# First Wk chunk loaded ahead of the third and fourth x tiles, with key matmuls of the first chunk between the transposes

## The chip, the cores and the metric

The kernel runs on one core of one Trainium2 chip. The metric is the device time of one execution in microseconds (us). The *span* in a profile is the time from the first to the last instruction of one execution; here it is about 2 us less than the device time of the same run.

## The reference, cut to what matters

```python
x = A_x                                          # 1 x 2048 x 512, bf16
g = sigmoid((x * gate_w).sum(-1))
a = linear_attention(x, wqkv, wo)                # 32 heads of 16; k = x @ Wk, pk = phi(k)
b = token_mlp(layernorm(x), w1, b1, w2, b2)      # mixes along the 2048 rows
out = g * a + (1 - g) * b
```

Only the start of the kernel matters here. It computes `k = x @ Wk` for the first row tiles of x. A tile is 128 rows, and there are 16. The contraction length of 512 is cut into four chunks of 128, so one tile needs four key matmuls, one per chunk of Wk, and all four need the tile transposed.

Of the kernel before, what the change touches and what calls it, by code (L numbers as in the profile page):

```python
# [15 lines left out]
def kernel(  # L16
# [13 lines left out]
    nc = tc.nc  # L30
# [10 lines left out]
    ND = D // P  # L41
# [25 lines left out]
    def bank(name, dtype=FP32):  # L67
        return ps.tile([P, SC], dtype, name=name, tag="bank")
# [39 lines left out]
    def mm(o, lhsT, rhs, start, stop, **kw):  # L108
        nc.tensor.matmul(o, lhsT=lhsT, rhs=rhs, start=start, stop=stop, **kw)  # L109
# [14 lines left out]
    def load_x(q, t0, n):  # L124
        q.dma_start(out=xs[:, t0 : t0 + n, :], in_=x_view[:, t0 : t0 + n, :])  # L125

    def load_wk(q, k):
        q.dma_start(out=wk_sb[:, k, :], in_=wqkv_view[:, k, D : 2 * D])
# [3 lines left out]
            out=xT[:, :, t0 * P : (t0 + n) * P], in_=X[t0 * P : (t0 + n) * P, :], transpose=True  # L132
        )

    for i in range(2):
        load_x(nc.sync, 2 * i, 1)
        load_x(nc.scalar, 2 * i + 1, 1)
    for i in range(2):
        load_wk(nc.sync, 2 * i)
        load_wk(nc.scalar, 2 * i + 1)  # L140
    NPE = 6
    load_x(nc.sync, 4, 2)
    for t0, n in ((NPE, 2), (8, 4), (12, 4)):
# [42 lines left out]
    def warm_up(n, cols=SC):  # L186
        for _ in range(n):
            mm(wps[:, :cols], warm[:, 0:P], warm[:, :cols], True, True)
# [5 lines left out]
    def transpose_tile(t, on_act):  # L194
        pt = bank("pt", BF16)
        for k in range(ND):
            nc.tensor.transpose(pt[:, k * P : (k + 1) * P], xs[:, t, k * P : (k + 1) * P], ident[:])  # L197
        dst = xT[:, :, t * P : (t + 1) * P]
        src = pt[:].rearrange("p (k s) -> p k s", k=ND)
        if on_act:  # L200
            nc.scalar.activation(out=dst, in_=src, func=ACT.Copy)
        else:
            nc.vector.tensor_copy(out=dst, in_=src)  # L203
# [13 lines left out]
    def k_part(t, ks):  # L217
        if t not in kaccs:
            kaccs[t] = bank("kacc")
        for k in ks:  # L220
            mm(
                kaccs[t][:], xT[:, k, t * P : (t + 1) * P], wk_sb[:, k, :],
                k == 0, k == ND - 1,
            )
# [4 lines left out]
    def ln_stats(t):  # L229
        stats = work.tile([P, nc.vector.BN_STATS_DIM], FP32, name="stats", tag="stats", bufs=2)  # L230
        nc.vector.bn_stats(out=stats[:], in_=xs[:, t, :])  # L231
        nc.vector.bn_aggr(out=mv[:, t, :], in_=stats[:])

    def ln_rstd(g):
        s = slice(g * TPC, (g + 1) * TPC)
        nc.vector.tensor_scalar_add(out=veps[:, s], in0=mv[:, s, 1], scalar1=EPS)
        nc.gpsimd.tensor_tensor(out=rstd[:, s], in0=veps[:, s], in1=mhalf[:], op=ALU.pow)
# [39 lines left out]
    def ln_step(u):  # L277
        ln_stats(u)
        if u % TPC == TPC - 1:
            ln_rstd(u // TPC)  # L280

    HEADS = 4
    transpose_tile(0, False)
    transpose_tile(1, True)
    warm_up(1, 256)
    transpose_tile(2, False)
    transpose_tile(3, True)
    ln_step(0)
    ln_step(1)
    for k in range(ND - 1):  # L290
        for t in range(HEADS):
            k_part(t, (k,))
    for t in range(HEADS):
        k_part(t, (ND - 1,))
        if t == 1:
# [210 lines left out]
```

## The kernel before: the parts that the change touches

```python
def load_x(q, t0, n): ...      # rows of x, 128 KB per tile
def load_wk(q, k): ...         # chunk k of Wk, 128 KB

for i in range(2):
    load_x(nc.sync, 2 * i, 1)          # SP queue:     x0, x2, wk0, wk2, then x4+x5, ...
    load_x(nc.scalar, 2 * i + 1, 1)    # scalar queue: x1, x3, wk1, wk3
for i in range(2):
    load_wk(nc.sync, 2 * i)
    load_wk(nc.scalar, 2 * i + 1)
load_x(nc.sync, 4, 2)
# ... all further loads on the SP queue

warm_up(6)                             # six 512-column matmuls on constants
HEADS = 4
transpose_tile(0, False)               # 4 transposes on PE, copy to xT by VectorE
transpose_tile(1, True)                # ... copy to xT by ScalarE
warm_up(1, 256)
transpose_tile(2, False)
transpose_tile(3, True)
ln_step(0); ln_step(1)                 # layernorm statistics, VectorE
for k in range(ND - 1):                # chunk-major: chunk 0 for tiles 0..3, chunk 1, chunk 2
    for t in range(HEADS):
        k_part(t, (k,))
for t in range(HEADS):                 # chunk 3
    k_part(t, (ND - 1,))
    if t == 1:
        transpose_tile(HEADS, False)
for t in range(HEADS):
    k_phi(t)                           # ScalarE exp, two VectorE operations -> pk
for t in range(HEADS, NT):
    k_part(t, range(ND))
    if t + 1 < NPE:                    # NPE = 6
        transpose_tile(t + 1, True)
    k_phi(t)
    g_tile(t - LAG)                    # 4 matmuls that use pk: "gacc" in the profile
    # ... layernorm pieces
```

I call the part up to the last of these first 16 key matmuls the *head*. The tile names in the profile are `wps` (warm-up), `pt` (transposes), `kacc` (key matmuls), `gacc` (the next matmuls, which use pk) and `zacc` (a short group of 16 matmuls after the last key tile). "Chunk 0" is `wk0` and "tile 3" is `x3`.

## Time and profile before

| | before |
|---|---|
| time, median of the first 3 runs | 168.21 us (167.87 to 168.40) |
| span of the profiled run | 166.4 us |
| PE busy | 97% of the span |
| wait of PE for the first Wk chunk | 0.41 us |
| first `gacc` matmul | 11.05 us |

The page of the kernel before gives the span, the busy time of each engine, and the chain of work that ended last by engine and by line:

```profile
span 166.4 us, 2105 instructions
...
PE 161.7 (97%) x806; PEld 74.9 (45%) x806; DVE 80.2 (48%) x190; ACT 59.0 (35%) x91; POOL 18.2 (11%) x37
...
PE 94%; DMA 3%; DVE 1%; SPq 0%; issue 0%
```

PE is the limit. The 3% DMA is at the very start. This is the timeline of PE alone; the columns are start, duration, engine, line, operation with tiles and shapes, count, and in brackets the idle time before the group and what ended it:

```profile
0.84 2.72 PE L109 MATMUL wps<-const-bfloat16-1.0 128*128 128x512 bf16 x6 [0.84 <-PEq L490]
3.62 1.03 PE L197 MATMUL pt<-ident,xs 128*128 128x128 bf16 x8
4.44 0.42 PE L109 MATMUL wps<-const-bfloat16-1.0 128*128 128x256 bf16 x1
4.66 0.96 PE L197 MATMUL pt<-ident,xs 128*128 128x128 bf16 x8
6.03 3.18 PE L109 MATMUL kacc<-wk_sb,xT 128*128 128x512 bf16 x14 [0.41 <-DMA wk_sb<-in_A_wqkv_dram]
...
11.05 1.23 PE L109 MATMUL gacc<-pk,xs 128*128 128x512 bf16 x4
```

All four tiles are transposed before the first key matmul. Then PE waits for chunk 0. From 6.03 the matmuls go out one every 0.216 us: the 14 of the group take 3.18 us, of which 0.38 is the last one's own duration, and (3.18 - 0.38) / 13 = 0.215. The chain of waits before says which load it was; the columns are start, duration and what:

```profile
1.72 4.26 DMA wk_sb<-in_A_wqkv_dram
5.99 0.04 issue
6.03 3.18 PE kacc L109 x14
```

Chunk 0 is third on the SP queue, is issued at 1.72 us and lands at 5.98 us.

### The profile page before, as it was taken

The numbers are of one execution on the slowest core, as the hardware profiler recorded it, in microseconds if no ns is written. First come the engines' busy times: TensorE is split into PE (matmuls) and PEld (weight loads), VectorE is DVE, ScalarE is ACT, GpSimd is POOL, SyncE is SP. The second block draws the span as 40 slices with busy tenths as digits, with TensorE's granted clock in tenths as the row PEclk, the third lists the DMA queues.
The fourth block names the chain that finished last, engine by engine and source line by source line (L and its number), as shares of the span: only waits on it lengthen the run. The fifth ranks groups of instructions, "written<-read, shape, count | busy, mean of one in ns | idle before, by whom it ended". The sixth has DMA issues, their size and how long they took to land.

```text
span 166.4 us, 2105 instructions
## 1 busy us (share of the span) xinstructions
PE 161.7 (97%) x806; PEld 74.9 (45%) x806; DVE 80.2 (48%) x190; ACT 59.0 (35%) x91; POOL 18.2 (11%) x37
## 2 busy tenths in 40 slices
PE   7999999999999999999999999999999999999992
PEld 3544444444544444444444444444444444444461
DVE  1569999986986769992301504051222121111121
ACT  3272474827658557222222111051111222111110
POOL 5000602100020000002712521000000000000000
PEclk9999999999999999999999999999999999999999
DMA  5999999999700001910597499931100000110001
GB/s 155 257 181 274 345 352 347 348 349 338 186 0 2 0 0 55 357 33 32 188 293 194 140 336 274 313 127 64 35 32 32 32 33 32 47 51 32 32 32 32
DMA packets 28953, 24.78 MB, mean 149 GB/s; under 512 B 6736, under 2 KB 28368, under 8 KB 28944
## 3 DMA queue, kind: packets, MB, share of 16 engines
q1 hardware_dynamic: 26928, 21.76, 45.0%
q0 software_dynamic: 1440, 2.38, 5.0%
q10 hardware_dynamic: 576, 0.52, 1.0%
q8 instruction: 6, 0.10, 0.3%
q14 instruction: 3, 0.02, 0.0%
HBM read 21.11 MB, written 2.23 MB: 140 GB/s over the span
## 4 chain that ended last, share of the span: by engine, by line
PE 94%; DMA 3%; DVE 1%; SPq 0%; issue 0%
PE uacc L109 29%; PE yps L109 29%; PE gacc L109 8%; PE qacc L109 8%; PE aps L109 8%; PE kacc L109 8%; DMA wk_sb<-in_A_wqkv_dram 3%; PE zacc L109 1%; PE denps L109 1%; PE kvps L109 1%; PE wps L109 1%; SPq L125 0%; DVE ot L471 0%; PE pt L197 0%; DVE xT L203 0%
## 5 line engine op out<-in xcount | busy, mean ns | idle before, releaser
L109 PE MATMUL uacc<-hs,w1c 128*128 128x512 bf16 x224 | 52.0, 379 | 0.0
L109 PE MATMUL yps<-uT,w2c 128*128 128x512 bf16 (+1 forms) x238 | 51.0, 367 | 0.0
L109 PEld LDWEIGHTS <-w2c 128*128 128x128 bf16 x238 | 23.3, 98 | 25.3
L109 PEld LDWEIGHTS <-w1c 128*128 128x128 bf16 x224 | 21.7, 98 | 26.3 <-issue 0.4
L471 DVE SCALAR_TENSOR_TENSOR ot<-yps,c,a_sc 128x512 bf16<-128x512 f32 (+1 forms) x17 | 12.1, 719 | 42.2 <-PE yps L109 41.2
L456 ACT ACTIVATE a_sc<-aps,c,gg 128x512 f32<-128x512 f32 x16 | 12.3, 777 | 46.8 <-PE aps L109 38.9
L418 DVE TENSOR_TENSOR pqT<-pqT,rex 128x512 bf16<-128x512 bf16 x16 | 6.6, 425 | 26.6 <-DMA rex<-rd_dram 26.5
L337 ACT ACTIVATE uT<-uacc,bcol 128x512 bf16<-128x512 f32 x14 | 9.3, 687 | 27.5 <-PE uacc L109 27.5
L109 PE MATMUL kacc<-wk_sb,xT 128*128 128x512 bf16 x64 | 16.1, 379 | 0.5 <-DMA wk_sb<-in_A_wqkv_dram 0.4
L109 PE MATMUL aps<-W2sb,pqT 128*128 128x512 bf16 x64 | 16.4, 379 | 0.0
L109 PE MATMUL qacc<-xT,wq_sb 128*128 128x512 bf16 x64 | 16.4, 379 | 0.0
L109 PE MATMUL gacc<-pk,xs 128*128 128x512 bf16 x64 | 16.1, 380 | 0.0
L247 ACT ACTIVATE hs<-xs,nmr,rstd 128x512 bf16<-128x512 bf16 x16 | 12.8, 804 | 2.5 <-DVE nmr L241 2.5
L207 ACT ACTIVATE e<-qacc 128x512 bf16<-128x512 f32 x16 | 9.6, 597 | 10.2 <-PE qacc L109 10.2
L207 ACT ACTIVATE e<-kacc 128x512 bf16<-128x512 f32 x16 | 9.1, 593 | 8.9 <-PE kacc L109 8.9
L208 DVE TENSOR_SCALAR e<-e 128x512 bf16<-128x512 bf16 x32 | 9.1, 284 | 6.3 <-ACT e L207 6.3
L211 DVE SCALAR_TENSOR_TENSOR pk<-kacc,e 128x512 bf16<-128x512 f32 x16 | 11.1, 692 | 0.6
L211 DVE SCALAR_TENSOR_TENSOR pqT<-qacc,e 128x512 bf16<-128x512 f32 x16 | 11.1, 692 | 0.5
L416 POOL DMA_DIRECT2D rex<-rd_dram x16 | 9.4, 597 | 16.6 <-DVE pqT L418 14.9
L231 DVE BATCH_NORM_STATS2 stats<-xs 128x6 f32<-128x512 bf16 x16 | 10.9, 682 | 0.0
L404 DVE CUSTOM_DVE_ANT_0 junk<-xs,gw_b 128x512 bf16<-128x512 bf16 x16 | 9.9, 688 | 0.0
L109 PEld LDWEIGHTS <-xT 128*128 128x128 bf16 x64 | 6.1, 98 | 8.2 <-issue 0.9
(66 smaller groups left out, 67.6 us busy)
## 6 DMA issues: line engine op xcount, KB each, us to landing
w2c<-in_B_w_dram SPq DMA_DIRECT2D x4, 1792.0 KB, 9.8
w1c<-in_B_w_dram SPq DMA_DIRECT2D x2, 2048.0 KB, 16.1
w1c<-in_B_w_dram SPq DMA_DIRECT2D x3, 1024.0 KB, 11.3
rex<-rd_dram POOLq DMA_DIRECT2D x16, 128.0 KB, 6.6
out_dram<-ot SPq DMA_DIRECT2D x15, 128.0 KB, 1.7
xs<-in_A_x_dram SPq DMA_DIRECT2D x2, 512.0 KB, 4.0
xs<-in_A_x_dram SPq DMA_DIRECT2D x2, 256.0 KB, 4.4
wq_sb<-in_A_wqkv_dram SPq DMA_DIRECT2D x1, 512.0 KB, 6.0
```

The costliest lines, as they stand in the source:

```text
L109: nc.tensor.matmul(o, lhsT=lhsT, rhs=rhs, start=start, stop=stop, **kw)
L207: nc.scalar.activation(out=e[:], in_=acc[:], func=ACT.Exp)
L208: nc.vector.tensor_scalar(out=e[:], in0=e[:], scalar1=1.0, scalar2=PHI_EPS, op0=ALU.min, op1=ALU.add)
L211: nc.vector.scalar_tensor_tensor(out=dst, in0=acc[:], scalar=0.0, in1=e[:], op0=ALU.max, op1=ALU.add)
L231: nc.vector.bn_stats(out=stats[:], in_=xs[:, t, :])
L247: nc.scalar.activation(out=hs[:, t, :], in_=xs[:, t, :], func=ACT.Identity, scale=rstd[:, t : t + 1], bias=nmr[:, t : t + 1],)
L337: nc.scalar.activation(out=uT[:, j, :], in_=acc[:], func=ACT.Gelu_apprx_tanh, bias=bcol[:, j : j + 1])
L404: nc.vector.tensor_tensor_reduce(out=junk[:], in0=xs[:, t, :], in1=gw_b[:], scale=1.0, scalar=0.0, op0=ALU.mult, op1=ALU.add, accum_out=gp ...
L416: nc.gpsimd.dma_start(out=rex[:], in_=src.unsqueeze(1).to_broadcast([8, HEAD, SC]))
L418: nc.vector.tensor_tensor(out=seg, in0=seg, in1=rex[:], op=ALU.mult)
L456: nc.scalar.activation(out=a_sc[:], in_=aps[:], func=ACT.Identity, scale=gg[:, t : t + 1], bias=c2[:, t : t + 1],)
L471: nc.vector.scalar_tensor_tensor(out=ot[:, :W], in0=yps[:, :W], scalar=c1[:, t : t + 1], in1=a_sc[:, cs], op0=ALU.mult, op1=ALU.add,)
```

## The change

The intent is to have PE do useful work in that wait. Chunk 0 is loaded second instead of third on the SP queue, tile 3 goes third there, and tile 2 takes second place on the scalar queue. On PE, two key matmuls of chunk 0 (tiles 0 and 1) come before tile 3's transposes, and the 256-column warm-up matmul is dropped.

```diff
-    for i in range(2):
-        load_x(nc.sync, 2 * i, 1)
-        load_x(nc.scalar, 2 * i + 1, 1)
-    for i in range(2):
-        load_wk(nc.sync, 2 * i)
-        load_wk(nc.scalar, 2 * i + 1)
+    load_x(nc.sync, 0, 1)
+    load_x(nc.scalar, 1, 1)
+    load_wk(nc.sync, 0)
+    load_x(nc.scalar, 2, 1)
+    load_x(nc.sync, 3, 1)
+    for k, q in ((1, nc.scalar), (2, nc.sync), (3, nc.scalar)):
+        load_wk(q, k)
@@
     transpose_tile(1, True)
-    warm_up(1, 256)
     transpose_tile(2, False)
+    ln_step(0)
+    k_part(0, (0,))
+    k_part(1, (0,))
     transpose_tile(3, True)
-    ln_step(0)
     ln_step(1)
-    for k in range(ND - 1):
-        for t in range(HEADS):
-            k_part(t, (k,))
+    k_part(2, (0,))
+    for t in range(3):
+        k_part(t, (1,))
+    k_part(3, (0, 1))
+    for t in range(HEADS):
+        k_part(t, (2,))
     for t in range(HEADS):
         k_part(t, (ND - 1,))
```

## The prediction

> **What bounds the kernel now.** The tensor engine. The page gives PE 97% busy of a 166.4 us span; the chain of waits is 94% PE, and its one long piece that is not PE is the first key-weight load (DMA wk_sb, 1.72 to 5.98 us). Timeline and waits of the first 13 us:
> - six warm-up matmuls until 3.56; tiles 0 and 1 transposed from 3.62, one 256-column warm-up matmul at 4.44, tiles 2 and 3 transposed 4.66 to 5.62;
> - PE idles 0.41 us for the first Wk chunk (landing at 5.99), then issues the 16 head key matmuls (4 tiles x 4 chunks) every 0.216 us, from 6.03 to about 9.49, without another wait.
> After this PE hardly stops, so what the head gains should reach the end undiminished. Only those 0.41 us and whatever PE does before 6.03 that is useless can be won.
>
> **What the change does.** No bytes and no useful work are added or removed. One warm-up matmul goes (0.21 us of issue time at the slow pace). On the SP queue chunk 0 moves from third to second place and x tile 3 from second to third; on the scalar queue tile 2 takes tile 3's second place. Chunks 1 to 3 keep their places. The Trainium skill, "DMA: Bandwidth & Descriptors", section "Issuing engines are not separate DMA queues", says that DMAs of all queues run on the same 16 engines and interleave. The trace agrees: the issues went out by 2.6 us, but tiles landed in pairs at about 3.6 to 3.8 and 4.2 to 4.4, and chunks at 6.0, 6.1, 6.6 and 6.9, at some 300 GB/s together. So the change trades landings: chunk 0 comes at about 4.5 to 5.0, tile 3 at about 5.4 to 6.0.
>
> **New head, estimated from these durations.** Tile 2 transposed by about 4.9; chunk 0 x tile 0 and x tile 1 (the latter needs the scalar engine's copy, done at 5.28) before about 5.7, perhaps at the slow pace, 0.43 us each; tile 3's transposes when it lands (0.2 to 0.4 us), its copy (0.60 us) hidden behind chunk 0 x tile 2 and chunk 1 x tiles 0 to 2; then everything back to back. At about 6.2, 14 key matmuls remain instead of 16 at 6.03. Two matmuls before the old start save 0.43 us; four transposes pushed past it give back 0.1 to 0.3. If tile 3 lands early, chunk 1 (still about 6.1) is the limit and 3 matmuls are ahead: at most about 0.55 us. Net: 0.25 us, all on the critical path. The head is only 2% of the span, so 2% cannot be won here.
>
> **Predicted:** 167.95 us, range 167.4 to 168.5. Faster by over 2%: 0.01; within 2%: 0.98; slower: 0.01.
>
> **What would show it.** Right: first key matmul at 4.9 to 5.2; chunk 0 about 1 us earlier; tile 3's transposes near 5.5 to 6.2, possibly after a PE wait for DMA xs; the first gacc matmul 0.1 to 0.5 us before 11.05; from there the same schedule, shifted. Wrong: chunk 0 still at about 6, or tile 3 after 6.3.
>
> **What would make it wrong.** The tensor clock. Matmuls until 4.86 took slow-clock times (0.63 us; transposes 0.31), those from 6.03 fast ones (0.38; later transposes 0.22). The skill, "TensorE: Matmul & The Clock Gate", Part 1, says that sustained activity over a window of about 3.4 us releases the clock, and that the window runs free. If the removed warm-up matmul or a wait for tile 3 makes a window count as idle, up to 3.4 us would run slowly: 8 key matmuls at about 0.43 instead of 0.216, an estimated loss of up to 1.7 us. Also run-to-run spread (0.5 us before) exceeds the gain.

## The result, and the profile after

| | before | after |
|---|---|---|
| time, median of 6 runs on one chip | 168.43 us (167.87 to 170.44) | 168.28 us (168.08 to 168.57) |
| ratio of fast runs, 95% interval | | 0.9999 (0.9981 to 1.0017) |
| span of the profiled run | 166.4 us | 166.5 us |
| first `gacc` matmul | 11.05 us | 11.15 us |

The 170.44 us of before lies over 1.5% above that kernel's fastest run (167.87), so it counts as slow; the five others have the median 168.40 us (up to 168.57). A ratio is the mean time of one kernel's fast runs over that of the other's in the same rounds, so it is not quite the ratio of the medians. Nothing can be told from noise here.

The chain on the page after has the same shares. Only the name of the load has changed, as its by-line entry shows:

```profile
PE 94%; DMA 3%; DVE 1%; SPq 0%; issue 0%
PE uacc L109 29%; PE yps L109 29%; PE gacc L109 8%; PE qacc L109 8%; PE aps L109 8%; PE kacc L109 8%; DMA xs<-in_A_x_dram 3%; PE denps L109 1%; PE zacc L109 1%; PE pt L198 1%; PE kvps L109 1%; PE wps L109 1%; DVE ot L476 0%; DVE xT L204 0%; SPq L128 0%; SPq L125 0%
```

The timeline of PE after:

```profile
3.45 1.46 PE L198 MATMUL pt<-ident,xs 128*128 128x128 bf16 x12
4.70 1.08 PE L109 MATMUL kacc<-wk_sb,xT 128*128 128x512 bf16 x2
6.24 0.48 PE L198 MATMUL pt<-ident,xs 128*128 128x128 bf16 x4 [0.46 <-DMA xs<-in_A_x_dram]
6.56 2.75 PE L109 MATMUL kacc<-wk_sb,xT 128*128 128x512 bf16 x12
...
11.15 1.23 PE L109 MATMUL gacc<-pk,xs 128*128 128x512 bf16 x4
```

And its chain of waits:

```profile
1.72 4.47 DMA xs<-in_A_x_dram
6.19 0.05 issue
6.24 0.48 PE pt L198 x4
```

The two early key matmuls are there, at 4.70. But PE now waits for tile 3. It is third on the SP queue, is issued at 1.72 exactly as chunk 0 was, and lands at 6.19. The books of this pair of profiles close:

- two matmuls done before the wait ended: 2 x 0.216 = 0.43 us saved;
- four transposes now behind the wait: 6.24 to 6.56 = 0.32 us given back;
- the awaited load landed later: 6.19 - 5.98 = 0.21 us given back;
- sum: 0.10 us lost, and the first `gacc` matmul is 0.10 us later (11.15 against 11.05).

From there both kernels run alike: span minus first `gacc` is 155.35 us in both.

### The profile page after: what moved, and what is told of

Same layout as the page of the kernel before. It is cut to its first block, busy times and chain, and to the rows that moved or that the text cites. A ratio compares the mean times of both kernels' runs of the same rounds, so it can differ in the third digit from the quotient of the medians.

```text
span 166.5 us, 2103 instructions
## 1 busy us (share of the span) xinstructions
PE 161.8 (97%) x805; PEld 74.6 (45%) x805; DVE 80.1 (48%) x190; ACT 59.0 (35%) x91; POOL 18.2 (11%) x37
## 4 chain that ended last, share of the span: by engine, by line
PE 94%; DMA 3%; DVE 1%; SPq 0%; issue 0%
PE uacc L109 29%; PE yps L109 29%; PE gacc L109 8%; PE qacc L109 8%; PE aps L109 8%; PE kacc L109 8%; DMA xs<-in_A_x_dram 3%; PE denps L109 1%; PE zacc L109 1%; PE pt L198 1%; PE kvps L109 1%; PE wps L109 1%; DVE ot L476 0%; DVE xT L204 0%; SPq L128 0%; SPq L125 0%
## 5 line engine op out<-in xcount | busy, mean ns | idle before, releaser
L109 PE MATMUL kacc<-wk_sb,xT 128*128 128x512 bf16 x64 | 16.7, 387 | 0.1
L109 PEld LDWEIGHTS <-wq_sb 128*128 128x128 bf16 x64 | 6.3, 98 | 7.6
```

The lines of the kernel that those rows point to most:

```text
L109: nc.tensor.matmul(o, lhsT=lhsT, rhs=rhs, start=start, stop=stop, **kw)
```

## The experiments

**Theory A.** What ends the wait of the head is whatever is third on a queue. It lands at about 6 us whether it is a strip of Wk or a tile of x. The change swaps one awaited load for another, gains the two matmuls done inside the wait, and pays with four transposes after it.

**Rivals.** N: the pair of profiles was unlucky, and a real gain of 0.25 us is hidden by noise. C: the clock ate the gain, because the early matmuls ran slowly and the warm-up matmul is gone. D: the new order on PE is what costs. E: rows of x come faster than strips of Wk. F: only the total of bytes counts, whatever the queue. G: what the head gains is taken back later.

Twelve runs were made, of ten kernels, and all were correct. Runs with five rounds have a ratio; the four single looks are of unknown state, and only their profiles are used. Runs 1 to 4 were on chip 2, the other timed runs on chip 1.

### 1. The kernel before against itself

No edit.

> The kernel before, unchanged, against itself: shows the spread of the comparison and gives a second profile. Both theories: ratio 1.000 within 0.2%. Theory A (the first key matmul waits for whatever lands third on its queue): the first chunk lands at 5.6 to 6.2 us again and the first gacc matmul starts at 10.8 to 11.3 us. Rival N (the profiles were an unlucky pair, and the gain of 0.25 us is real): the first gacc matmul later than in the repeated profile of after by 0.2 us or more.

Measured: 168.25 us, ratio 0.9992 (0.9974 to 1.0010). Chunk 0 landed at 6.07 and the first `gacc` matmul started at 11.15. So 0.1 us in the head is the profile's own scatter, and about 0.2% is the limit of the timing.

### 2. The changed kernel again

No edit.

> The changed kernel, unchanged, a second profile and more times. Theory A: x tile 3 lands at 5.8 to 6.4 us, PE stands idle 0.4 to 0.9 us before its transposes, first gacc matmul within 0.15 us of the kernel before; ratio 0.999 to 1.001. Rival N (noise hid a gain): tile 3 lands before 5.8, first gacc matmul 0.2 us or more before that of the kernel before, ratio at or under 0.9985.

Measured: 168.19 us, ratio 0.9985 (0.9968 to 1.0003). The timeline of PE:

```profile
4.71 0.82 PE L109 MATMUL kacc<-wk_sb,xT 128*128 128x512 bf16 x2
6.23 0.40 PE L198 MATMUL pt<-ident,xs 128*128 128x128 bf16 x4 [0.69 <-DMA xs<-in_A_x_dram]
6.46 2.75 PE L109 MATMUL kacc<-wk_sb,xT 128*128 128x512 bf16 x12
...
11.05 0.59 PE L109 MATMUL gacc<-pk,xs 128*128 128x512 bf16 x2
11.90 0.38 PE L109 MATMUL gacc<-pk,xs 128*128 128x512 bf16 x1 [0.25 <-ACT xT L202]
```

Tile 3 landed at 6.18. Against the repeated profile of before: 0.43 saved, 0.23 for the transposes (6.23 to 6.46), 0.11 for the landing; sum 0.09 won, and the first `gacc` matmul is 0.10 us earlier (11.05 against 11.15). The same account gave +0.10 in the first pair and gives -0.10 here. The ratio lies just under the 0.999 that theory A expected and exactly at rival N's mark of 0.9985, which is a gain of 0.25 us. So the times cannot tell the forecast gain from none; they leave no room for 0.5%. What speaks against N is the profile: tile 3 landed at 6.18 and not before 5.8, and the first `gacc` matmul came 0.10 us earlier and not 0.2 or more.

### 3. New order of the loads, old order on PE

```diff
 # the kernel before, with
-    for i in range(2): ...            # x0 x1 x2 x3, then the chunks
+    load_x(nc.sync, 0, 1)             # the seven lines of the change
+    ...
```

> New order of the loads, old order on PE (all four tiles transposed before any key matmul, warm-up kept). Theory A (the wait has moved from the first chunk to tile 3, and the only profit is the two key matmuls done while waiting): tile 3 lands at about 6.2 us, PE waits for it, all 16 head matmuls come after it, first gacc matmul at about 11.5, which is 0.4 later than in after (two matmuls of 0.216 us) and 0.5 later than before; ratio about 1.002 to 1.003. Rival C (what ate the gain is the slow clock of the early matmuls or the missing warm-up): no worse than after, ratio about 1.000 or under.

Measured: 168.63 us, ratio 1.0010 (0.9990 to 1.0029). The timeline of PE:

```profile
6.01 0.40 PE L198 MATMUL pt<-ident,xs 128*128 128x128 bf16 x4 [1.38 <-DMA xs<-in_A_x_dram]
6.25 3.40 PE L109 MATMUL kacc<-wk_sb,xT 128*128 128x512 bf16 x14
...
11.49 0.59 PE L109 MATMUL gacc<-pk,xs 128*128 128x512 bf16 x2
```

PE stands idle 1.38 us and starts all 16 key matmuls after it. The first `gacc` matmul is 0.44 us later than in run 2. That is not the two matmuls alone: 0.43 for them, plus 0.22 because tile 3's copy (0.60 us on ScalarE) is no longer hidden (14 matmuls take 3.40 us here instead of 3.18), minus 0.22 because tile 3 was reached earlier (6.01 against 6.23). Rival C expected no loss and is wrong on this point: the matmuls inside the wait are worth their full time. The ratio is lower than the expected 1.002, and its interval touches it.

### 4. Old order of the loads, new order on PE

```diff
 # the changed kernel, with
-    load_x(nc.sync, 0, 1)             # the seven lines of the change
-    ...
+    for i in range(2): ...            # x0 x1 x2 x3, then the chunks
```

> Old order of the loads, new order on PE. Theory A: the first chunk lands third again, at about 6.0 us; chunk 0 x tiles 0 and 1 wait for it although tile 3 has been there since 4.3; tile 3's transposes (about 0.22 to 0.32 us) now stand after the wait; first gacc matmul at about 11.3, 0.25 later than before; ratio about 1.001 to 1.002. Rival D (the new order on PE is what costs, the loads are fine): first gacc clearly later than 11.4.

Measured: 168.59 us, ratio 1.0022 (0.9991 to 1.0053). Chunk 0, third again, landed at 5.86. The timeline of PE:

```profile
5.91 0.59 PE L109 MATMUL kacc<-wk_sb,xT 128*128 128x512 bf16 x2 [1.34 <-DMA wk_sb<-in_A_wqkv_dram]
6.34 0.39 PE L197 MATMUL pt<-ident,xs 128*128 128x128 bf16 x4
6.56 2.76 PE L109 MATMUL kacc<-wk_sb,xT 128*128 128x512 bf16 x12
...
11.16 0.59 PE L109 MATMUL gacc<-pk,xs 128*128 128x512 bf16 x2
```

Two key matmuls come first, then the four transposes from 6.34 to 6.56 (0.22 us), then the other key matmuls. From landing to first `gacc` it took 5.30 us, against 5.07 in the first profile of before: the 0.22 of the transposes. The new order on PE costs only that, so rival D is wrong; each half of the change alone gains nothing.

### 5. A third matmul inside the wait

Chunk 0 x tile 2 has its operands by 5.4 us, yet in the changed kernel it stands behind tile 3's transposes, and PE keeps its order. Moved ahead:

```diff
     transpose_tile(2, False)
     ln_step(0)
-    k_part(0, (0,))
-    k_part(1, (0,))
+    for t in range(3):
+        k_part(t, (0,))
     transpose_tile(3, True)
     ln_step(1)
-    k_part(2, (0,))
-    for t in range(3):
-        k_part(t, (1,))
-    k_part(3, (0, 1))
-    for t in range(HEADS):
-        k_part(t, (2,))
+    for k in (1, 2):
+        for t in range(3):
+            k_part(t, (k,))
+    k_part(3, (0, 1, 2))
```

It ran twice, first as a single look:

> After, with the matmul of chunk 0 x tile 2 moved ahead of tile 3's transposes (its operands are there by 5.4 us), and tile 3's matmuls of chunks 1 and 2 moved behind those of the other tiles. Theory A (nothing but the work done inside the wait for the third landing counts): tile 3 lands at 5.9 to 6.2 us, 13 head matmuls remain instead of 14, first gacc matmul 0.22 us earlier than in after, at 10.8 to 10.95; span 166.15 to 166.3. Rival C (slow clock or missing warm-up decide): no change, first gacc matmul at 11.05 to 11.15.

Measured: span 166.0, first `gacc` at 10.67, both better than expected; tile 3 landed at 5.80, before the expected 5.9 to 6.2. PE, busy with the three matmuls at the slow pace, reached its transposes only at 6.03, so here the landing was not what it waited for.

Then with five rounds:

> The version with the third matmul inside the wait (as the single look before, now timed). Theory A: first gacc matmul at 10.65 to 10.9, 0.2 to 0.45 before that of the kernel before, all of which reaches the end: ratio 0.9970 to 0.9988. Rival N (differences this small in the head don't show in the time of the program): ratio 0.9995 to 1.0005.

Measured: 167.98 us against 168.49, ratio **0.9965 (0.9949 to 0.9982)**. The timeline of PE:

```profile
4.66 1.14 PE L109 MATMUL kacc<-wk_sb,xT 128*128 128x512 bf16 x3
5.63 0.39 PE L198 MATMUL pt<-ident,xs 128*128 128x128 bf16 x4
5.86 2.54 PE L109 MATMUL kacc<-wk_sb,xT 128*128 128x512 bf16 x11
...
10.24 1.22 PE L109 MATMUL gacc<-pk,xs 128*128 128x512 bf16 x4
```

Tile 3 landed early here, at 5.58, so part of the profile's lead is luck. From the start of its transposes to the first `gacc` it is 10.24 - 5.63 = 4.61 us, against 4.82 in run 2 (11.05 - 6.23): the 0.21 us of one matmul. The time is better than that of before by an interval that excludes 1. This is the only version of which that can be said. The ratio is a little better than the expected 0.9970 to 0.9988. It was not timed beside the changed kernel: against before, the intervals of the two overlap (0.9949 to 0.9982 and 0.9968 to 1.0003), so that the third matmul beats the change is shown by the profiles alone.

### 6. A filler matmul in the wait

```diff
     k_part(1, (0,))
+    warm_up(2, 256)
     transpose_tile(3, True)
```

> After, with two 256-column warm-up matmuls between the second key matmul and tile 3's transposes, so inside the wait: tests the clock. Theory A: the landing of tile 3 decides, and the two early key matmuls at the slow clock lay wholly inside the wait; the filler changes at most the pace of tile 3's transposes (0.1 us at most); first gacc matmul at 11.0 to 11.2, ratio to before 0.9985 to 1.001. Rival C (the removed warm-up matmul cost the gain through a later clock release): gain of 0.2 us or more, first gacc matmul at or under 10.9.

Measured: 168.30 us, ratio 0.9992 (0.9971 to 1.0014). The first `gacc` matmul was at 10.60, which taken alone would be rival C's sign. But in this profile tile 3 landed at 5.73. From the start of its transposes (5.77) to the first `gacc` it took 4.83 us, against 4.82 in run 2: nothing was gained by the filler. The ratio is no better than that of the changed kernel. A profile's head can be compared only after the landing has been taken out.

This profile could not test the clock, though. The trace's record of full clock begins at 4.22 us, before the filler began (5.39), and its transposes took 0.22 to 0.23 us from 4.26 on. But all 14 profiles have this record. Full clock began at 4.04 to 6.18 us (mean 5.06) in the six that keep the 256-column warm-up matmul and at 3.80 to 6.70 us (mean 5.23) in the eight without it. So the start of full clock differs by almost 3 us from profile to profile, and no effect of that matmul shows in it.

### 7. Two chunks ahead of tiles 2 and 3

```diff
     load_wk(nc.sync, 0)
-    load_x(nc.scalar, 2, 1)
-    load_x(nc.sync, 3, 1)
-    for k, q in ((1, nc.scalar), (2, nc.sync), (3, nc.scalar)): ...
+    load_wk(nc.scalar, 1)
+    load_x(nc.sync, 2, 1)
+    load_x(nc.scalar, 3, 1)
+    load_wk(nc.sync, 2)
+    load_wk(nc.scalar, 3)
 # and on PE: chunks 0 and 1 x tiles 0 and 1, then transposes of tiles 2 and 3, then the rest
```

> The change taken one step further: chunks 0 and 1 second on the two queues, x tiles 2 and 3 third. Theory A, place on the queue decides and not what is loaded: chunks 0 and 1 land by about 4.3 us, tiles 2 and 3 both at 5.9 to 6.3; four key matmuls are done in the wait (they save 4 x 0.216 = 0.86 us), but eight transposes follow it (0.43 to 0.6 us), and chunk 2 (about 6.9) may hold up the rest by 0.1 to 0.3: first gacc matmul at 10.85 to 11.15, so no clear gain over after. Rival E (x rows, whole in memory, come faster than the strips of Wk): tiles 2 and 3 land before 5.5.

Measured: both chunks landed by 4.3 us, tiles 2 and 3, now third, at 5.78 and 5.98. First `gacc` at 11.21, span 166.6; it was 0.06 us later than the latest that I had expected. The timeline of PE:

```profile
4.58 2.06 PE L109 MATMUL kacc<-wk_sb,xT 128*128 128x512 bf16 x4
6.43 0.74 PE L199 MATMUL pt<-ident,xs 128*128 128x128 bf16 x8
7.01 2.36 PE L109 MATMUL kacc<-wk_sb,xT 128*128 128x512 bf16 x10
```

PE did not wait for the tiles: full clock began only at 6.70 us in this profile, the last early matmuls went out 0.40 to 0.43 us apart, and PE reached the transposes at 6.43, 0.45 us after the later tile had landed. So here part of rival C is true, and the run does not show what two early chunks are worth at full clock. It does test rival E, which is wrong: x tiles in third place came at 5.78 and 5.98, not before 5.5.

### 8. Chunk 0 on a third queue

```diff
 # the kernel before, with
+    load_wk(nc.gpsimd, 0)
     for i in range(2):
         load_x(nc.sync, 2 * i, 1)
         load_x(nc.scalar, 2 * i + 1, 1)
-    for i in range(2): ...
+    load_wk(nc.scalar, 1)
+    load_wk(nc.sync, 2)
+    load_wk(nc.scalar, 3)
```

> The kernel before, with chunk 0 loaded from the GpSimd queue as that engine's first work; everything else in its old order, so chunk 1 moves up on the scalar queue's third place and chunk 2 to the third place of the SP queue. Theory A (the third place on a queue lands late because five or six 128 KB loads share the engines and a few of the sixteen shares come late): chunk 0 now is first on its queue and lands at 3.8 to 5.0 us, tiles 0 to 3 land up to 0.4 us later than before; the wait for chunk 0 (0.41 us) goes and the head matmuls start at 5.4 to 5.8: first gacc matmul 10.5 to 10.9, span 165.9 to 166.3. Rival F (the loads are limited by the total of bytes alone, whatever the queue): chunk 0 lands no earlier than 5.5, or the tiles are as much later as it is earlier: first gacc matmul at 11.0 or later.

Measured as a single look: chunk 0 landed at 5.45, later than the 5.0 expected; first `gacc` at 10.51 and span 165.9, as expected. It looked like the best version. Timed:

> Chunk 0 on the GpSimd queue, old order elsewhere, now timed. Theory A: first gacc matmul at 10.4 to 10.7, span 0.4 to 0.6 shorter than before; ratio 0.9960 to 0.9978. Rival N: 0.9995 to 1.0005.

Measured: 168.30 us, ratio 0.9993 (0.9971 to 1.0015). In this second profile it was a tile of x that came late, as its chain of waits shows, although it was second on the scalar queue:

```profile
1.24 4.09 DMA xs<-in_A_x_dram
5.33 0.05 issue
5.38 0.40 PE pt L198 x4
```

The first `gacc` matmul was at 10.85, 0.34 us later than in the single look. The ratio missed the expected 0.9960 to 0.9978, though its interval reaches 0.9971; that the single look was lucky in its landings fits both profiles and is not shown beyond them. The Trainium skill, "DMA: Bandwidth & Descriptors", section "Rules for kernel authors", says that spreading loads over the SP, ACT and GpSimd queues doesn't help bandwidth, because all run on the same 16 engines. The traces agree: from 2.8 to 7.0 us they show 288 GB/s in the kernel before, and 284 and 286 GB/s in the two profiles with the third queue.

Rival F is not excluded. Chunk 0 was first on its queue here, but the fifth load to be issued (at 1.33 us), and it landed at 5.45, at 5.08, and in run 10 at 5.57. In the eleven profiles of the two-queue order, the load that was third on the SP queue was also the fifth of all (issued at 1.72 or 1.73). No run separates the place on a queue from the number of loads issued before.

### 9. The copies of tiles 4 and 5 hidden

In run 2 above, the fourth `gacc` matmul is put down as waiting for the copy of tile 5. It starts 0.20 us late (the record of the third is missing from the trace, which makes it 0.25 in the line). PE also loses 0.25 us to the copy of tile 4. In this run both tiles are transposed earlier, inside the last row of the head, with both copies on VectorE:

```diff
+    transpose_tile(HEADS, False)
     for t in range(HEADS):
         k_part(t, (ND - 1,))
-        if t == 1:
-            transpose_tile(HEADS, False)
+        if t == 0:
+            transpose_tile(HEADS + 1, False)
@@
-        if t + 1 < NPE:
-            transpose_tile(t + 1, True)
```

> After, with the transposes of tiles 4 and 5 moved up into the head's last row of matmuls and both copies on the vector engine. Nothing is changed in the loads. In every profile so far PE loses about 0.25 us waiting for the copy of tile 4 and about 0.2 us for that of tile 5. Theory A (PE is the limit from the head to the end, so any PE wait removed anywhere in it comes out at the end whole): span shorter than after by 0.35 to 0.45, 165.95 to 166.1. Rival G (what is won in the head is taken back by a later wait for loads or for the vector engine): span 166.3 to 166.5.

Measured: span 166.2, where theory A expected at most 166.1 and rival G at least 166.3. By the key matmuls of tile 5, PE was 0.49 us ahead of run 2 (11.63 against 12.12), of which 0.25 came from an earlier landing of tile 3 (5.93 against 6.18). At the z matmuls it lost 0.26 us, as the timeline of PE shows:

```profile
32.44 1.31 PE L109 MATMUL zacc<-pk,zsel 128*32 128x512 bf16 x16
```

In run 2 the same line reads

```profile
32.93 1.05 PE L109 MATMUL zacc<-pk,zsel 128*32 128x512 bf16 x16
```

The last z matmul needs the last pk from VectorE, which was done at 33.32 us. The stretches of the kernel before show why VectorE is there no sooner; the columns are the stretch, its length, then busy time with count of PE, PEld, DVE, ACT and POOL, then granted clock, DMA share and GB/s:

```profile
9.50:32.00 22.50, 22.38 (x107) 10.05 (x106) 21.60 (x54) 13.80 (x24) 3.94 (x5) 1.00 1.05 311
```

VectorE is busy 21.60 of 22.50 us, though the page's share of the whole span is 48%. From the first phi to the z matmuls there are two full chains, PE and VectorE. Rival G is right here: without the earlier landing PE was 0.24 us ahead, and 0.26 us went at the z matmuls. The edit also gave VectorE one copy more (0.43 us, before on ScalarE) just before its first phi, which started only 0.18 us earlier than in run 2 (9.63 against 9.81); with that copy left on ScalarE the loss might be smaller, which was not tried. For the change itself rival G doesn't hold, since its head moves both chains.

### 10. Both chains earlier

Chunk 0 on the GpSimd queue as in run 8, the copies of tiles 4 and 5 both on VectorE as in run 9, and tile 0 finished first so that VectorE's chain starts sooner:

```diff
-    for k in range(ND - 1):
+    for k in range(2):
         for t in range(HEADS):
             k_part(t, (k,))
     for t in range(HEADS):
-        k_part(t, (ND - 1,))
-        if t == 1:
-            transpose_tile(HEADS, False)
+        k_part(t, (2, 3))
+        if t == 0:
+            transpose_tile(HEADS, False)
+            transpose_tile(HEADS + 1, False)
@@
-        if t + 1 < NPE:
-            transpose_tile(t + 1, True)
```

> Chunk 0 on the GpSimd queue, and besides: after the rows of chunks 0 and 1, tile 0 gets chunks 2 and 3 first, then tiles 4 and 5 are transposed (both copies on the vector engine), then tiles 1 to 3 get chunks 2 and 3. In the run with hidden copies PE came earlier by 0.4 us but then waited 0.33 us at the z matmuls for the vector engine's last pk, because the vector engine works without a break from the first phi to that point. Theory H (two chains of nearly the same length, PE and the vector engine, run from the head to the z matmuls; a gain has to start both earlier): the first phi on the vector engine starts at 8.6 to 8.9 instead of 9.3, no wait at the z matmuls, span 165.4 to 165.6, ratio 0.9940 to 0.9960. Rival I (hiding the copies is worth nothing whatever the vector engine does): span as with the third queue alone, 165.8 to 166.0, ratio 0.996 to 0.998.

Measured: in the profile the first phi on VectorE started at 8.87, the z matmuls took 1.05 us again, and the span was 165.6: as theory H expected.

```profile
8.87 0.28 DVE L209 TENSOR_SCALAR e<-e 128x512 bf16<-128x512 bf16 x1
32.05 1.05 PE L109 MATMUL zacc<-pk,zsel 128*32 128x512 bf16 x16
```
Against run 8's single look, whose key matmuls began 0.12 us earlier (5.49 against 5.61), it ended 0.3 us sooner. But the times don't bear out the expected 0.9940 to 0.9960. The ratio is 1.0009 (0.9969 to 1.0048), and one of the six runs was slow (170.35 us at a granted clock of 0.987); with that run the ratio of the plain means is 0.9998. The mean of its five fast runs, 168.14, over the mean of the 11 runs of before, 168.54, is 0.9976; the spans of its other four fast runs are 166.1 or 166.2. So theory H is shown for one profile, and the gain in time is inconclusive.

### What the landings did

The chains and the trace's landing counts give the landing of the load that was third on the SP queue in the eleven profiles of runs with a plain two-queue order:

| third on the SP queue | landing, us |
|---|---|
| chunk 0 | 5.98, 6.07, 5.86 |
| x tile 3 (x tile 2 in run 7) | 6.19, 6.18, 5.97, 5.80, 5.58, 5.73, 5.93, and 5.78 |

The means are 5.97 and 5.90: no effect of what is loaded shows. One profile differs from another by up to 0.6 us, two profiles of one kernel by at most 0.22. The four on chip 2 are at 5.86 to 6.18, the three on chip 14 at 5.78 to 5.93, the two on chip 1 at 5.58 and 5.73, so chip and chance cannot be told apart. Taking the landing out, the time from it to the first `gacc` matmul compares the orders on PE:

| kernel | landing to first `gacc`, us |
|---|---|
| before (two profiles) | 5.07, 5.08 |
| new loads, old PE order | 5.52 |
| old loads, new PE order | 5.30 |
| after (two profiles) | 4.96, 4.87 |
| after, third matmul in the wait (two profiles; in the first, PE came 0.23 us after the landing) | 4.87, 4.66 |

At an equal landing the change is therefore worth 0.11 to 0.21 us, about 0.1% of 168 us; the lower figure is from the profile whose transposes ran partly at the slow pace (0.32 against 0.23 us). With the third matmul it is up to 0.42 us (5.08 - 4.66), 0.25%, inside the interval of run 5. The landing's own scatter, 0.6 us, is larger than either.

Why the third load takes so long is partly visible. The trace counts 16 shares of each load, one per DMA engine. These are the times (us) of the 16 counts of chunk 0 before, and of tile 3 after:

```
before, chunk 0: 4.38 4.42 4.57 4.58 4.60 4.66 4.74 4.81 4.83 4.88 4.89 5.09 5.20 5.47 5.50 5.99
after,  tile 3:  4.30 4.32 4.33 4.35 4.36 4.38 4.49 4.53 4.58 4.68 5.09 5.31 5.32 5.81 6.14 6.19
```

Most of the load is there by 5.1 us, and the last few shares come up to 1.1 us later. The Trainium skill, "DMA: Bandwidth & Descriptors", section "Why a DMA increments its semaphore by 16 and not by 1", says that the engines finish independently and that only the full 16 means that all data has landed; the counts show the first of these, with 1.6 and 1.9 us between first and last. Why some engines fall behind was not tried and stays open.

## Why the prediction was right or wrong

The measured 168.28 us lies in the range and "within 2%" was right, but neither tests the mechanism: the range, 167.4 to 168.5, also holds the time of the kernel before (168.21 and 168.40). The forecast gain of 0.25 us was not seen, and the spread of the times could have hidden it. The step that was off is the landing of tile 3: the prediction had 14 key matmuls left at about 6.2 us, and they were left at 6.56 and 6.46. Point by point:

- *PE bounds the kernel, and what the head gains reaches the end undiminished.* Right for the change: span minus first `gacc` is 155.3 to 155.4 us in the profiles of before, after and runs 3 and 5. Too simple in general: run 9 moved PE alone and lost 0.26 us to VectorE at the z matmuls.
- *Chunk 0 comes at about 4.5 to 5.0.* Right in kind, too cautious: it landed at 4.03 (4.08 in run 2), and the first key matmul began at 4.70 instead of 4.9 to 5.2.
- *Tile 3 at about 5.4 to 6.0.* This term was mis-sized. It landed at 6.19 and 6.18 in the two profiles of the changed kernel (in the six others with an x tile there at 5.58 to 5.97, inside the range), and over all runs at about the same time as chunk 0 in that place (means 5.90 and 5.97). I had reasoned that landings would be traded, and yet let tile 3 come earlier than the load whose place it took.
- *Two matmuls save 0.43; four transposes give back 0.1 to 0.3.* Right: 0.43, and 0.32 and 0.23 measured. With no gain from the landing the sum is 0.11 to 0.20, not 0.25; with the landings as they fell (0.21 and 0.11 later) it is +0.10 and -0.09.
- *First `gacc` 0.1 to 0.5 us before 11.05.* Wrong in both profiles: 11.15 and 11.05.
- *The clock as the main risk.* It did not cost the 1.7 us. The Trainium skill, "TensorE: Matmul & The Clock Gate", Part 1, has the clock released after a window of sustained activity that runs free; the traces agree in so far as full clock began anywhere from 3.80 to 6.70 us. In the changed kernel the two early matmuls took 0.61 to 0.63 us each at the slow pace in the first profile, inside the wait where it costs nothing, and those from 6.56 on took 0.38 us. A trace of it is in the transposes: 0.32 us where two of them still ran slowly, 0.23 in the second profile. In run 7 the slow pace outlasted the wait and cost more.
- *Spread exceeds the gain.* Right: 0.5 us or more, and run 1 against itself gave 0.9992 with an interval 0.36% wide.

## What to carry to other kernels

When a load is moved up, ask which load takes the place that it leaves, and what will wait for that one: here whatever stood in that place landed at 5.6 to 6.2 us. The gain is then only the work that can be done inside the wait, minus the work that was pushed behind it; put all the ready work there before the first instruction that must wait (a third matmul was worth 0.21 us more, and that version alone was clearly faster than before, by 0.35% with an interval from 0.18 to 0.51%). Compare such small changes after taking the scatter of the landing out, and look where the clock was released; never go by the span of one profile: the filler and the third queue each looked 0.5 us better in one profile (165.9 against 166.4) and gave 0.9992 and 0.9993 when timed.

## What the Trainium skill lacked or had wrong

- "DMA: Bandwidth & Descriptors" fits the time of one DMA issued from GpSimd with a fixed cost and a bandwidth. It doesn't say how far apart the shares of one load land when several loads from the SP and scalar queues are in flight: 1.1 to 1.9 us between first and last of 16 here for the load third on the SP queue, and 5.58 to 6.19 us for its landing from profile to profile. That scatter is larger than the gains compared here.
- "TensorE: Matmul & The Clock Gate", section "Back-to-back issue gap", gives about 131 ns per matmul of 512 columns for a real stream of weight loads and matmuls. Here they went out every 215 ns at the full granted clock, which is what its formula for the isolated gap gives.
- The same page, Part 4, says that the fast clock doesn't engage for transposes. Here the slow transposes took 0.31 us each and the later ones 0.22 us, four of them in 0.39 us (9.05 us in the profile of before). The trace calls them MATMUL and doesn't show the mode.
